# Block-local attention: every other step issued in reverse order on TensorE

## Chip, cores, metric

One core of a Trainium2 chip. The metric is the device time of one execution in microseconds (us). TensorE multiplies matrices (its weight load is a separate instruction), VectorE and ScalarE and GpSimd work on elements, and SyncE only issues the DMAs. In the rows PE is TensorE, PEld its weight loads, DVE is VectorE, ACT is ScalarE, POOL is GpSimd, SP is SyncE and SPq its queue of DMA issues. Each engine works through its own instructions strictly in the order of the program and waits for others by semaphores.

## What is computed

An attention layer is followed by two feed-forward layers; only the attention is touched. Shapes: 2 batches, 8 heads, 768 positions, 64 channels per head.

```python
k_sum = k.reshape(B, H, nb, block, D).max(axis=3)        # 24 blocks of 32
v_sum = v.reshape(B, H, nb, block, D).mean(axis=3)
scores_l = scale * q @ k^T, kept where |i - j| < 16, else -1e9
scores_s = scale * q @ k_sum^T + log(32)
a = softmax(concat(scores_l, scores_s))
x = a @ concat(v, v_sum)                                  # -> 1536 tokens x 512
x = moe(x)      # h = x @ w_in;  (h * cos h) @ w_out
return moe2(x)  # h = x @ w_in2; (h * softmax h), layer norm, @ w_out2
```

## The kernel before

Attention runs over 8 pairs of heads (pair n), and each pair over 3 groups of queries, so there are 24 groups G = 3n + g. A group is four tiles of 64 queries for both heads of its pair; a tile meets a window of 96 keys and the 24 block columns, 120 columns (KW) in all. The loop `for step in range(NGR + LA)` (29 steps) is a software pipeline written by hand: in one step each engine works on another stage of another group, and the order of the Python lines is the order on each engine.

In step t TensorE issues, in this order: the scores of group t+1 (`emit_s`, L507; 16 products of 64 rows by 64 columns, two at a time), the transposes of the weights of group t-4 (`emit_t`, L544; 4 of 128 by 128), when g = 2 the transposes of k and q of pair n+2 (L443, L479), from step 15 on three or four products of the first feed-forward layer (`fill`, L234), the products with v of group t-5 (`emit_av`, L562; 16 of 120 rows by 64 columns), and in steps 1, 2, 4, 7, 10, 13, 16, 19 the block sums of v of a pair (`sum_v`, L421; 24 of 96 rows by 64 columns).

VectorE in step t does the softmax sum of group t-2, when g = 0 the block maxima of k (L455), the masked maximum of group t (`emit_max`, L518), the last part of a weight conversion (`weights.finish`, L171), and when g = 1 copies of k and q (`pair_k`, `pair_q`, L375). GpSimd does `weights.split` (L187), the subtraction of the maximum (L522), the normalisation of group t-2 (L537), and the low half of a chunk of X (`split_x`, L204). ScalarE does the high half of a weight block (L186), the exponential of group t-1 (L527), the first part of a weight conversion (`weights.rebias`, L163 and L164), the copy of the transposed weights out of PSUM (`emit_at`, L552), the copy of the group's result to X (`emit_x`, L576), when g = 0 the key and query layouts of the next pair (`emit_kx`, `emit_qx`, L464 to L493), the high half of `split_x` (L203), and the scaling of the block sums (`scale_v`, L429). From group 20 (copy of weights) and 19 (copy to X) on, the two copies are VectorE's.

SyncE's queue gets in a step: the loads of weight blocks (`weights.bits`, L139, in the steps of `WSTEPS`, each one block ahead), when g = 1 the loads of k and q of pair n+3 and of v of pair n+2 (`load_v`, four DMAs, L389 and L393), and one step after `sum_v` the DMAs that put the block means beside v (`place_vsum`, L436). The weight block asked for in step 9 is the first one.

Four buffers hold v ("vt"), so `load_v(4)` in step 7 takes the buffer of pair 0 and `load_v(6)` in step 13 that of pair 2; its DMAs wait until the last product with v of that pair, groups 2 and 8. `emit_s` uses two PSUM banks in turn, `emit_t` one bank, `emit_av` one bank, which the copies give free. The block sums of pairs 6 and 7 use the PSUM space of the transposes of k and q. After step 28 TensorE goes on with the feed-forward layers; the products of the first of them need chunks of X that `split_x` makes in the steps of `XS`.

Of the kernel before, what the change touches and what calls it, by code (L numbers as in the profile page):

```python
# [7 lines left out]
F32 = mybir.dt.float32  # L8
# [12 lines left out]
QT = 64  # L21
# [13 lines left out]
def fused_kernel(  # L35
# [15 lines left out]
    P = 128  # L51
# [7 lines left out]
    KW = WIN + NS  # L59
    NG = 4  # L60
# [25 lines left out]
    def bank(i, name):  # L86
        return ps.tile([P, 512], F32, tag=f"m{i}", name=name)
# [4 lines left out]
    wide = w_in.dtype == mybir.dt.int64  # L92
    LOWEST = -3.0e38
    WSTEPS = (9, 10, 12, 13, 15, 17, 18, 19)
    XS = (7, 10, 13, 16)
    IDLE = (0, 0, 0)
    DVE_AT = 20
    DVE_X = 19
# [201 lines left out]
    def warm_up(n):  # L300

        if not n:
            return
        t = ps_h0.tile([P, 512], F32, tag="h", name="idle")
        for _ in range(n):
            nc.tensor.matmul(t, lhsT=idle[:, 0:P], rhs=idle, start=True, stop=True)
# [28 lines left out]
    def attention():  # L335
        st = ExitStack()
        with st:
            io = st.enter_context(tc.tile_pool(name="io", bufs=2))
            fix = st.enter_context(tc.tile_pool(name="fix", bufs=1))
            sm_p = st.enter_context(tc.tile_pool(name="sm", bufs=6))  # L340
# [24 lines left out]
            def load_k(n):  # L365
                k_t[n] = load_heads(k, n, "kt", 2)
# [11 lines left out]
            def pair_k(n):  # L378
                k_t[n] = side_by_side(k_t[n], "kg", False)

            def pair_q(n):
                q_t[n] = side_by_side(q_t[n], "qg", n < 2)
# [27 lines left out]
            def blocks_of(t):  # L410
                at = FIRST if t == 0 else FINAL if t == NT - 1 else MID + 2 * HALF - 2 * (t % HALF)
                return strip[0:WIN, at:at + D]

            def sum_v(n):

                o = (ps_h0 if n < 6 else ps_qk).tile(
                    [P, 512] if n < 6 else [P, 2, 2, S // 2], F32, tag="h" if n < 6 else "qk", name="vsum")
                o = (o if n < 6 else o[:, 0, 0])[:, 0:P]
                for t in range(HALF):
                    for c in range(2):  # L420
                        nc.tensor.matmul(  # L421
                            o[D * c:D * c + D], lhsT=blocks_of(HALF * c + t),
                            rhs=v_t[n][0:WIN, HALF * c + t].rearrange("p j d -> p (j d)"),
                            start=(t == 0), stop=(t == HALF - 1))
                vs_t[n] = o
# [21 lines left out]
            def emit_k(n):  # L447
                qk = ps_qk.tile([P, 2, 2, S // 2], F32, tag="qk", name="qk")
                transposed(k_t.pop(n), qk[:, 0, 0], qk[:, 0, 1])
                qk_t["k", n] = qk[:, 0]  # L450
                qk_t["q", n] = qk[:, 1, 0], qk[:, 1, 1]
# [45 lines left out]
            sm_t, at_t, ss_t, o_t, sum_t = {}, {}, {}, {}, {}  # L497

            def emit_s(G):
                n, g = divmod(G, GPP)  # L500
                qx, kx = kx_t[n]
                sps = bank(G % 2, "sps").rearrange("p (i s) -> p i s", i=NG)[:, :, 0:KW]
                for i in range(NG):
                    t = NG * g + i
                    for j in range(2):
                        h = slice(D * j, D * j + D)
                        nc.tensor.matmul(  # L507
                            sps[h, i, :], lhsT=qx[h, t * QT:(t + 1) * QT], rhs=kx[h, t, :],
                            start=True, stop=True)
                ss_t[G] = sps  # L510

            def emit_max(G):
                g = G % GPP
                sm = sm_t[G] = sms[G % NSM]
                sps = ss_t.pop(G)
                mx = sm_p.tile([P, NG], F32, tag="mx", name="mx")
                for i in range(NG):
                    nc.vector.tensor_tensor_reduce(  # L518
                        out=sm[:, i, 0:KW], in0=sps[:, i, :], in1=mask[:, g + i, :], scale=1.0, scalar=LOWEST,
                        op0=ALU.add, op1=ALU.max, accum_out=mx[:, i:i + 1])  # L520
                sm = sm[:, :, 0:KW]
                nc.gpsimd.tensor_tensor(  # L522
                    out=sm, in0=sm, in1=mx.unsqueeze(2).to_broadcast([P, NG, KW]), op=ALU.subtract)
# [21 lines left out]
                at_t[G] = aps  # L545

            def emit_at(G):
                at = sm_p.tile([KW, NG, P], F32, tag="at", name="at", bufs=2)
                if G >= DVE_AT:
                    nc.vector.tensor_copy(at, at_t[G])  # L550
                else:
                    nc.scalar.activation(out=at, in_=at_t[G], func=AF.Copy)  # L552
                at_t[G] = at

            def emit_av(G):
                n, g = divmod(G, GPP)
                b, hp = divmod(n, NP)
                at, vt = at_t.pop(G), v_t[n]
                ops = bank(3, "ops").rearrange("p (i s) -> p i s", i=NG)[:, :, 0:QT]
                for i in range(NG):  # L560
                    for j in range(2):
                        nc.tensor.matmul(  # L562
                            ops[64 * j:64 * j + 64, i, :], lhsT=vt[0:KW, NG * g + i, j, :],
                            rhs=at[:, i, 64 * j:64 * j + 64], start=True, stop=True)
                o_t[G] = ops

            def emit_x(G):
                n, g = divmod(G, GPP)
                b, hp = divmod(n, NP)
                ops = o_t.pop(G)  # L570
                c0 = b * S + g * NG * QT
                dst = X[:, hp, c0:c0 + NG * QT].rearrange("p (i s) -> p i s", i=NG)
                if G >= DVE_X:
                    nc.vector.tensor_copy(dst, ops)
                else:
                    nc.scalar.activation(out=dst, in_=ops, func=AF.Copy)  # L576

            NPAIR = B * NP
            NGR = NPAIR * GPP
# [25 lines left out]
            LX, LN, LT, LA = 1, 2, 4, 5  # L605
            VSUM_AT = {1: 0, 2: 1, **{3 * m - 2: m for m in range(2, NPAIR)}}
            for step in range(NGR + LA):
                n, g = divmod(step, GPP)
                summed = LN <= step < NGR + LN
                ahead = n + 1 if g == 0 and n + 1 < NPAIR else 0  # L610

                warm_up(IDLE[g] if step < min(FILL) else 0)
                if step + 1 < NGR:
                    emit_s(step + 1)
                if step == 0:
                    emit_max(0)
                    pair_k(1)
                    pair_q(1)
                    emit_k(1)
                    emit_q(1)  # L620
                if LT <= step < NGR + LT:
                    emit_t(step - LT)
                if g == 2 and n + 2 < NPAIR:
                    emit_k(n + 2)
                    emit_q(n + 2)
                fill(step)
                if step >= LA:
                    emit_av(step - LA)
                if step in VSUM_AT:
                    sum_v(VSUM_AT[step])  # L630

                weights.split()
                if LX <= step < NGR + LX:
                    emit_exp(step - LX)
                if summed:
                    emit_sum(step - LN)
                if ahead and step:
                    emit_ksum(ahead)
                weights.rebias()
                if 0 < step < NGR:  # L640
                    emit_max(step)
                if ahead and not step:
                    emit_ksum(ahead)
                drain(step - NGR)
                if LT <= step < NGR + LT:
                    emit_at(step - LT)
                weights.finish()
                if summed:
                    emit_norm(step - LN)
                if step >= LA:  # L650
                    emit_x(step - LA)
                if ahead:
                    emit_kx(ahead)
                    emit_qx(ahead)
                if step in WSTEPS:
                    weights.bits()
                for c in range(KC):
                    if step == XS[c]:
                        xs_of[0, c] = split_x(0, c, xs_a)
                if g == 1 and n + 2 < NPAIR:  # L660
                    pair_k(n + 2)
                    pair_q(n + 2)

                if g == 1 and n + 3 < NPAIR:
                    load_k(n + 3)
                    load_q(n + 3)
                if g == 1 and n + 2 < NPAIR:
                    load_v(n + 2)
                if step - 1 in VSUM_AT:
                    place_vsum(VSUM_AT[step - 1])  # L670
                if step in VSUM_AT:
                    scale_v(VSUM_AT[step])
# [303 lines left out]
```

## Time and profile before

| what | us |
|---|---|
| median of 3 runs (lowest to highest) | 494.49 (492.2 to 495.02) |
| the profiled execution | 492.56 |
| its span on the core | 490.8 |
| TensorE busy in the span | 477.8 (97%) |
| attention, up to the first product of `emit_y` (L276) | 103.0 |
| feed-forward layers behind it | 387.8 |

The busy time says how much of the span an engine had an instruction at work. From 103 us on TensorE has hardly a gap; all else that it lacks lies in the attention stage, where four engines and the DMA queues hand work to each other. So the stage has to be read by its waits, step by step: the timeline of each engine there, and the chain of waits that ended last.

### The profile page before, as it was taken

The numbers are of one execution on the slowest core, as the hardware profiler recorded it, in microseconds if no ns is written. First come the engines' busy times: TensorE is split into PE (matmuls) and PEld (weight loads), VectorE is DVE, ScalarE is ACT, GpSimd is POOL, SyncE is SP. The second block draws the span as 40 slices with busy tenths as digits, with TensorE's granted clock in tenths as the row PEclk, the third lists the DMA queues.
The fourth block names the chain that finished last, engine by engine and source line by source line (L and its number), as shares of the span: only waits on it lengthen the run. The fifth ranks groups of instructions, "written<-read, shape, count | busy, mean of one in ns | idle before, by whom it ended". The sixth has DMA issues, their size and how long they took to land.

```text
span 490.8 us, 7868 instructions
## 1 busy us (share of the span) xinstructions
PE 477.8 (97%) x2938; PEld 392.4 (80%) x2938; DVE 299.8 (61%) x667; ACT 314.1 (64%) x540; POOL 149.8 (31%) x144
## 2 busy tenths in 40 slices
PE   8899799999999999999999999999999999999997
PEld 4787687778888888888888888888888888888886
DVE  3895876773455456556564664556477776776661
ACT  3578889646685766556656653788624867777621
POOL 0586998622422222222222220245500011110000
PEclk9999999999999999999999999999999999999999
DMA  8888872201223322332233221220001333224201
GB/s 248 204 220 252 235 191 58 106 2 43 87 85 97 118 85 87 92 124 85 85 98 116 87 85 39 90 87 1 0 1 43 87 87 86 66 64 65 70 37 44
DMA packets 59046, 46.17 MB, mean 94 GB/s; under 512 B 40448, under 2 KB 51328, under 8 KB 59008
## 3 DMA queue, kind: packets, MB, share of 16 engines
q1 hardware_dynamic: 59008, 45.67, 32.4%
q8 instruction: 23, 0.38, 0.3%
q14 instruction: 15, 0.12, 0.1%
HBM read 36.61 MB, written 3.15 MB: 81 GB/s over the span
## 4 chain that ended last, share of the span: by engine, by line
PE 87%; ACT 3%; POOL 3%; DVE 3%; DMA 2%; issue 1%; SPq 0%; ACTq 0%; POOLq 0%
PE y L276 27%; PE h L234 26%; PE o L851 13%; PE h L737 13%; PE sps L507 2%; PE ops L562 1%; PE aps L544 1%; POOL sm L522 1%; PE vsum L421 1%; DMA qt<-in_q_dram 1%; DMA raw<-in_moe_w_in_dram 1%; POOL sm L537 1%; POOL w L187 1%; ACT kx L464 1%; PE qk L443 1%
## 5 line engine op out<-in xcount | busy, mean ns | idle before, releaser
L234 PE MATMUL h<-xs,w 128*128 128x512 f32 x576 | 141.2, 391 | 0.0
L276 PE MATMUL y<-gs,w 128*128 128x512 f32 x576 | 138.2, 389 | 0.0
L276 PEld LDWEIGHTS y<-gs,w 128*128 128x128 f32 x576 | 108.0, 188 | 22.5
L234 PEld LDWEIGHTS h<-xs,w 128*128 128x128 f32 x576 | 107.1, 188 | 21.6
L187 POOL TENSOR_TENSOR w<-s,w 128x512 fp32r<-128x512 f32 x48 | 62.5, 1302 | 157.8 <-ACT w L186 134.8
L243 ACT ACTIVATE r<-h 128x512 int32<-128x512 f32 x48 | 28.6, 596 | 85.9 <-PE h L234 85.9
L248 DVE SCALAR_TENSOR_TENSOR r<-r,h 128x512 f32<-128x512 int32 x48 | 32.9, 685 | 67.2 <-ACT r L243 67.1
L171 DVE SCALAR_TENSOR_TENSOR s<-raw 128x512 int32<-128x512 int32 x48 | 36.7, 764 | 52.3 <-ACT raw L164 44.1
L851 PE MATMUL o<-w,ls 128*128 128x512 f32 (+1 forms) x312 | 67.8, 373 | 0.0
L737 PE MATMUL h<-w,xs 128*128 128x512 f32 x288 | 67.6, 390 | 0.0
L851 PEld LDWEIGHTS o<-w,ls 128*128 128x128 f32 x312 | 55.3, 188 | 10.7 <-DVE ls L827 0.4
L737 PEld LDWEIGHTS h<-w,xs 128*128 128x128 f32 x288 | 53.9, 188 | 11.1
L204 POOL TENSOR_TENSOR xs<-X,xs 128x512 fp32r<-128x512 f32 x22 | 30.6, 1398 | 37.6 <-ACT xs L203 37.6
L772 POOL TENSOR_TENSOR st<-st,mhalf 128x1 f32<-128x1 f32 x12 | 6.6, 550 | 110.1 <-DVE st L771 100.0
L253 ACT ACTIVATE r<-r,half_pi 128x512 f32<-128x512 f32 x48 | 34.5, 718 | 1.6 <-DVE r L248 1.6
L264 DVE TENSOR_TENSOR gs<-h,gs 128x512 fp32r<-128x512 f32 x48 | 32.6, 679 | 4.2 <-ACT gs L263 4.0
L258 DVE TENSOR_TENSOR h<-h,r 128x512 f32<-128x512 f32 x48 | 32.9, 685 | 0.4 <-ACT r L253 0.4
L163 ACT ACTIVATE raw<-raw 128x512 f32<-128x512 f32 x48 | 31.8, 662 | 0.6 <-DMA raw<-in_moe_w_in_dram 0.6
L164 ACT ACTIVATE raw<-raw 128x512 int32<-128x512 uint32 x48 | 31.8, 663 | 0.0
L522 POOL TENSOR_TENSOR sm<-sm,mx 128x480 f32<-128x480 f32 x24 | 25.6, 1065 | 19.4 <-DVE mx L518 19.4
L186 ACT ACTIVATE w<-s 128x512 fp32r<-128x512 f32 x48 | 30.1, 626 | 1.8 <-DVE s L171 1.5
L754 ACT ACTIVATE e<-h,st 128x1024 f32<-128x1024 f32 (+1 forms) x13 | 13.6, 1049 | 26.3 <-DVE st L750 22.9
(79 smaller groups left out, 560.9 us busy)
## 6 DMA issues: line engine op xcount, KB each, us to landing
raw<-in_moe_w_in_dram SPq DMA_DIRECT2D x24, 512.0 KB, 3.9
raw<-in_moe_w_out_dram SPq DMA_DIRECT2D x24, 512.0 KB, 3.3
vt<-in_v_dram SPq DMA_DIRECT2D x16, 240.0 KB, 4.9
kt<-in_k_dram SPq DMA_DIRECT2D x8, 384.0 KB, 3.7
qt<-in_q_dram SPq DMA_DIRECT2D x8, 384.0 KB, 4.0
out_dram<-osb SPq DMA_DIRECT2D x11, 256.0 KB, 2.0
vt<-vm SPq DMA_DIRECT2D x16, 72.0 KB
vt<-in_v_dram SPq DMA_DIRECT2D x16, 48.0 KB, 5.6
```

What stands on the lines that cost most here:

```text
L163: nc.scalar.activation(out=hw, in_=hw, func=AF.Prelu, scale=REBIAS, alpha=NEGATIVE)
L164: nc.scalar.activation(out=lw, in_=lw.bitcast(U32), func=AF.Copy, scale=TOP3)
L171: nc.vector.scalar_tensor_tensor(out=self.f32[i], in0=t[:, :, 1], scalar=3, in1=t[:, :, 0], op0=ALU.logical_shift_left, op1=ALU.bitwise_or)
L187: nc.gpsimd.tensor_tensor(out=w[:, 1, :], in0=f, in1=as32(w[:, 0, :]), op=ALU.subtract)
L234: nc.tensor.matmul(h, lhsT=w[:, a, f * P:(f + 1) * P], rhs=xs_of[tb, c][:, b_, :], start=(m == 0), stop=(m == 3 * KC - 1))
L248: nc.vector.scalar_tensor_tensor(out=r, in0=r.bitcast(I32), scalar=TWO_PI, in1=h_of[step], op0=ALU.mult, op1=ALU.subtract)
L253: nc.scalar.activation(out=r, in_=r, func=AF.Sin, scale=-1.0, bias=half_pi)
L258: nc.vector.tensor_tensor(out=h, in0=h, in1=r, op=ALU.mult)
L264: nc.vector.tensor_tensor(out=gs[:, 1, :], in0=r, in1=as32(gs[:, 0, :]), op=ALU.subtract)
L276: nc.tensor.matmul(y[e], lhsT=w[:, a, e * P:(e + 1) * P], rhs=gs[:, b_, :], start=(f == 0 and i == 0), stop=(f == GF - 1 and i == 2))
L737: nc.tensor.matmul(banks[n], lhsT=xs_of[NTB + t // TPB, c][:, a, t0:t0 + P], rhs=weights.done[w2i[c][n]][:, b_, :], start=(m == 0), stop=( ...
L851: nc.tensor.matmul(o, lhsT=ls_of[t][f // 4][:, a, s0:s0 + P], rhs=w[:, b_, cols], start=(f == 0 and i == 0), stop=(f == NF2 - 1 and i == 2))
```

## The change

Even steps keep their order on TensorE, odd steps run it backwards, and the products with v of two groups are issued together in the even step. Even step t: scores of t+1, transposes of t-4, (k and q), fill, products with v of t-6 and of t-5, block sums. Odd step t: block sums, transposes of t-4, (k and q), fill, scores of t+1. The results of two groups share one PSUM bank, and both are copied to X in the odd step that follows (`emit_x`). The transposed weights get a third buffer. Two chunks of X are split one step later (`XS`).

```diff
-    XS = (7, 10, 13, 16)
+    XS = (7, 11, 13, 17)
...
-                at = sm_p.tile([KW, NG, P], F32, tag="at", name="at", bufs=2)
+                at = sm_p.tile([KW, NG, P], F32, tag="at", name="at", bufs=3)
...
-                ops = bank(3, "ops").rearrange("p (i s) -> p i s", i=NG)[:, :, 0:QT]
+                if G % 2 == 0:
+                    o_t["bank"] = bank(3, "ops").rearrange("p (a i s) -> p a i s", a=2, i=NG)
+                ops = o_t["bank"][:, G % 2]
...
-                if step + 1 < NGR:
+                odd = step % 2
+                if step + 1 < NGR and not odd:
                     emit_s(step + 1)
+                if odd and step in VSUM_AT:
+                    sum_v(VSUM_AT[step])
...
                 fill(step)
-                if step >= LA:
+                if odd and step + 1 < NGR:
+                    emit_s(step + 1)
+                if not odd and step > LA:
+                    emit_av(step - LA - 1)
                     emit_av(step - LA)
-                if step in VSUM_AT:
+                if not odd and step in VSUM_AT:
                     sum_v(VSUM_AT[step])
...
-                if step >= LA:
-                    emit_x(step - LA)
+                if step > LA and (odd or step == NGR + LA - 1):
+                    end = step - LA + 1 - odd
+                    emit_x(end - 2)
+                    emit_x(end - 1)
```

## Rows read from the trace of the kernel before

**Rows 1.** Busy time by stretch: us, each engine (instructions), PEclk, DMA share, GB/s

```profile
110.00:135.00 25.00, 25.00 (x112) 20.68 (x112) 10.71 (x16) 17.07 (x32) 8.32 (x7) 1.00 0.20 64
```

**Rows 2.** Chain of waits, in order of time: start us, us, what

```profile
39.82 3.90 DMA raw<-in_moe_w_in_dram
...
86.19 1.04 PE sps L507 x16
...
102.96 5.67 PE y L276 x24
```

**Rows 3.** Timeline of TensorE, steps 3 to 8: start us, us, instruction, [idle before]

```profile
21.43 1.86 PE L507 MATMUL sps<-kx,qx 64*64 64x120 f32 x32
...
28.74 1.04 PE L507 MATMUL sps<-kx,qx 64*64 64x120 f32 x16
29.71 0.65 PE L544 MATMUL aps<-ident,sm 128*120 128x128 f32 x4
30.29 0.69 PE L562 MATMUL ops<-at,vt 120*64 120x64 f32 x16
30.90 1.04 PE L507 MATMUL sps<-kx,qx 64*64 64x120 f32 x16
...
32.97 1.48 PE L421 MATMUL vsum<-vt,strip 96*64 96x128 f32 x24
...
37.24 0.69 PE L562 MATMUL ops<-at,vt 120*64 120x64 f32 x16
```

**Rows 4.** Timeline of SyncE's issues, 28 to 40 us

```profile
28.26 1.73 SPq L393 DMA_DIRECT2D vt<-in_v_dram  x1
...
33.18 0.34 SPq L389 DMA_DIRECT2D vt<-in_v_dram  x1
...
38.10 1.67 SPq L436 DMA_DIRECT2D vt<-vm  x2
39.82 1.50 SPq L139 DMA_DIRECT2D raw<-in_moe_w_in_dram  x3
```

**Rows 5.** View of the tile vt: from issue of its DMAs to landing

```profile
DMA to landing us min/median/max: 3.4/5.5/6.8
```

**Rows 6.** DMA issues of the page: KB each, median us from issue to landing

```profile
raw<-in_moe_w_in_dram SPq DMA_DIRECT2D x24, 512.0 KB, 3.9
...
qt<-in_q_dram SPq DMA_DIRECT2D x8, 384.0 KB, 4.0
```

**Rows 7.** Timeline of SyncE's issues, 66 to 69 us

```profile
66.61 0.32 SPq L389 DMA_DIRECT2D vt<-in_v_dram  x1
...
68.73 0.40 SPq L139 DMA_DIRECT2D raw<-in_moe_w_out_dram  x1
```

**Rows 8.** Timeline of ScalarE, 43 to 78 us

```profile
43.74 0.67 ACT L163 ACTIVATE raw<-raw 128x512 f32<-128x512 f32 x1 [0.56 <-DMA raw<-in_moe_w_in_dram]
...
63.58 0.38 ACT L576 ACTIVATE X<-ops 128x256 f32<-128x256 f32 x1 [0.47 <-PE ops L562]
...
72.14 0.38 ACT L576 ACTIVATE X<-ops 128x256 f32<-128x256 f32 x1 [1.45 <-PE ops L562]
...
76.74 0.82 ACT L493 ACTIVATE qx<-qk 128x768 f32<-128x768 f32 x1
```

**Rows 9.** Timeline of GpSimd at 46 us

```profile
46.31 1.46 POOL L204 TENSOR_TENSOR xs<-X,xs 128x512 fp32r<-128x512 f32 x1 [3.23 <-ACT xs L203]
```

**Rows 10.** Timeline of VectorE, the maximum of group 20

```profile
81.64 0.28 DVE L518 CUSTOM_DVE_ANT_0 sm<-sps,mask 128x120 f32<-128x120 f32 x1
```

**Rows 11.** Timeline of VectorE, steps 24 to 27

```profile
93.64 0.42 DVE L574 COPY X<-ops 128x256 f32<-128x256 f32 x1 [0.86 <-PE ops L562]
...
101.11 0.68 DVE L550 COPY at<-aps 120x512 f32<-120x512 f32 x1
```

**Rows 12.** Timeline of VectorE, two copies of q

```profile
46.06 0.55 DVE L375 COPY qg<-qt 128x768 f32<-128x768 f32 x1
...
57.30 1.63 DVE L375 COPY qg<-qt 128x768 f32<-128x768 f32 x1
```

## The prediction

> **What bounds the kernel now.** I read the busy time by stretch first: from 110 us on TensorE is busy for the whole of a stretch [rows 1], and the attention stage ends where the first product of the feed-forward layer starts, at 102.96 [rows 2]. The change touches only what lies before, so its gain or loss is the shift of that point. Then the chain of waits of that stage: it does not stay on one engine. Up to 38 us it runs on TensorE, there it goes through SyncE's queue to the load of the first weight block [rows 2], then over ScalarE, GpSimd and VectorE, and it comes back to TensorE at 86.19 with the scores of group 23 [rows 2]. So time taken out of TensorE counts in full at the start and at the end of the stage, and in the middle only where TensorE is what the others wait for.
>
> **The price of a change of product.** Two groups of scores side by side are busy for 1.86 us, one for 1.04 [rows 3]: the second costs 0.82. Alone, scores occupy TensorE from 28.74 to 29.71, 0.97. The difference, 0.15 us, is what one change of kind costs. Products with v take 0.61 (30.29 to 30.90) and I take the same 0.15 for a second group of them, so 0.46. Before, two steps have six changes (scores, transposes, v, twice); after, four. I count 10 new pairs of scores (groups 2 and 3 wait for a layout in any case, 4 and 5 stand side by side already) and 12 pairs of products with v: 22 times 0.15 is 3.3 us of TensorE's work. It is the most that the change can give, if every bit lies on the path.
>
> **The first stretch, to step 8: nothing is left.** Four of the pairs lie here (-0.6). But in step 7 the block sums of pair 3 now come first. Before, they start at 32.97 without waiting, two blocks of products after the step's start at 30.90 [rows 3]. The last DMA of that v is issued at 28.26 [rows 4] and takes at least 3.4 us [rows 5], so it lands at 31.66 at the earliest; TensorE comes to it at some 30.9 and waits 0.8 or more (32.97 bounds it: 2.1). That takes back the 0.6. I take +0.1 for TensorE here.
>
> **SyncE's queue: the one moved wait.** `load_v(4)` of step 7 needs the buffer of pair 0, and the last reader of it, group 2's products with v, goes from step 7 to step 8. Before, the load starts at 33.18, right when they end [rows 4]. After, they stand in front of those of group 3, which start at 37.24 [rows 3]; without group 2's own 0.61 in step 7, and with half a block of them to run, and the +0.1, they end at 37.2 to 37.9. I take 37.9: the load comes 4.7 us later. Behind it on the queue are `place_vsum(3)`, which nobody needs soon, and then the first weight block, which ScalarE does need. Before, the queue went from 33.18 to 39.82 in 6.6 us: 4.9 for the four DMAs of v, then 1.7 [rows 4]. The four are that slow because the queue was still full: the load of q just ahead takes 4.0 us to land [rows 6]. With the queue empty, the same four took 66.61 to 68.73, 2.1 us [rows 7]. The loads of k and q ahead are issued before 33.18 and so land by 37.2, and at 37.9 the queue is empty: 37.9 + 2.1 + 1.7 = 41.7 for the weight block against 39.82, **+1.9** (bounds: +1.4 if they end at 37.4; +4.7 if the queue takes 6.6 again). ScalarE stood ready 0.56 before the block landed at 43.72 [rows 8], so all of the delay is its idle time, and the other engines hang on it from here: GpSimd already stands 3.23 us before, waiting for ScalarE [rows 9]. Two effects hide in this shadow at no cost: the block sums of pair 5, now first in step 13, wait for a v that comes later too, where TensorE anyway waits for ScalarE; if that cover were thin, +0.7. `load_v(6)` moves likewise from step 13 to 14; the weight blocks behind it are each a block ahead, and its v is wanted only at the end of step 16: nothing.
>
> **XS.** The second chunk's split moves from step 10 to 11. On GpSimd it took 1.46 us in that idle time [rows 9]; in step 11 it stands in front of a weight block's low half and the next maximum. Between 0 and 1.46; I take half, **+0.7**. The fourth chunk (16 to 17) delays fill in step 18 on TensorE, which is idle shortly after: nothing.
>
> **ScalarE's waits for products with v.** Before, its copy to X waits for products of the same step: 0.47 at 63.58 and 1.45 at 72.14, where TensorE has k, q and fill in front [rows 8]. After, the copies come one step behind the products and wait for nothing: **-1.9**, in steps where ScalarE has nothing else free. Waits like these before 43 us don't count, as ScalarE then waits for the weight block.
>
> **Step 19.** Block sums of pair 7 now come first and need the space that `emit_qx(7)` frees at 77.56 (76.74 + 0.82) [rows 8]. TensorE comes to them some 2.2 us sooner than before, the time of one step's scores, transposes and products with v (28.74 to 30.90) [rows 3], stands as long, then needs 1.5 for the sums, 0.6 and 1.0 for transposes and scores: group 20's scores end at 80.6. They are wanted at 81.64 [rows 10]: hidden, by 1.0 us. If not, up to +1.5.
>
> **The end of the stage.** From 86.19 four pairs of products with v save 0.6. But VectorE's chain of the activation bounds these steps too, down to the last copy of weights at 101.11; its copy of group 19, which waited 0.86 for TensorE at 93.64 [rows 11], leaves step 24, and those of 20 and 21 leave steps 25 and 26. Between 0 and -1.5; I take **-0.7**.
>
> **Sum.** +0.1 + 1.9 + 0.7 - 1.9 - 0.7 = +0.1 us on the profiled execution's own 492.56 (span 490.8, 1.8 around it). That execution lies 1.9 under the median of the runs, 494.49, and I set the forecast beside the median: **494.5 us**, with its own range from 492.5 to 496.5 from the terms' bounds.
>
> **Rivals.**
>
> A. *All of TensorE's saving arrives* (-3.0 of the 3.3): the late weight block is made up in steps 10 to 18 by ScalarE and TensorE together. For it: TensorE is without a gap in long parts of the stage. Against: the chain leaves it between 39 and 86 us. 491.5.
>
> B. *The weight block comes 4.7 late, not 1.9*: slower. The place is SyncE's queue in step 8, the price the 4.9 us for four DMAs [rows 4] instead of 2.1 [rows 7], so +2.8; it decides as soon as these issues take over 4 us. Against it stands the empty queue, for it that only the last of the eight loads of v went that quickly. 497.3.
>
> C. *VectorE's copies of q lose their place to GpSimd.* In step 10 one takes 0.55, started just ahead of GpSimd's work; in step 13, with GpSimd at work, 1.63 [rows 12]. The change shifts both engines against each other; if the two quick ones of steps 10 and 16 become slow, two times 1.08 lies on VectorE's queue ahead of weight conversion: +2.2, 496.7. The Trainium skill has this as a rule (Advanced Engine Details and Errata, VectorE Performance Modes: VectorE's second port is GpSimd's too, and copies that use it and GpSimd's instructions block each other); the trace agrees by 0.55 and 1.63.
>
> D. *The change doesn't do what it says.* The second scores of a pair wait for the maximum two groups back, the second transposes for the copy of the first, with only products with v or a fill between: if such waits part the pairs, the saving of the last stretch falls away and some is lost. 495.7.
>
> **How the numbers follow.** Forecast 0.48, A 0.13, B 0.16, C 0.12, D 0.11. About 0.5%, 2.5 us, is what a measurement of this kernel can tell from no change. Faster (under 492.0): most of A and a little of the forecast's edge, 0.13. Slower (over 497.0): most of B and under half of C, 0.18. Same: 0.69. The range holds the forecast's, C and D and half of A and B: 491.4 to 497.6.
>
> **What would show it.** Right: scores in pairs of 1.86 us and products with v in pairs near 1.15; `load_v(4)` at about 37.9 and the first weight load at about 41.7; ScalarE's wait for it near 2.4 instead of 0.56; no wait of its copies to X for TensorE; TensorE standing some 2 us ahead of the last block sums; the first product of `emit_y` within 1.5 us of 102.96. Wrong: the weight block's load before 40.5 or after 43; scores in step 20 later than 81.6; over 1 us of waits of transposes for copies in steps 23 to 28, which I have priced at nothing. Anything that differs behind 103 us would be outside this reasoning.

## The result, and the profile after

| what | before | after |
|---|---|---|
| median of 7 runs (lowest to highest), us | 495.02 (491.98 to 495.62) | 497.26 (496.10 to 501.12) |
| ratio to before, 95% interval | | 1.0077 (1.0055 to 1.0100) |
| the profiled execution, us | 492.56 | 496.10 |
| its span, us | 490.8 | 494.3 |
| first weight conversion on ScalarE (L163) starts at | 43.74 | 47.41 |
| first product of `emit_y` in the chain of waits at | 102.96 | 106.46 |
| feed-forward layers behind it (span less the line above) | 387.8 | 387.8 |

The change makes the kernel slower, by more than 0.5%. (The medians of the seven runs are 2.2 us apart, their means, 497.94 and 494.25, 3.7; the ratio rests on all the runs.) Medians here and below are of all runs of a kernel; ratios leave out one run of e9_late_weights, 798.03 us at a granted clock of 0.56.

In the two profiled executions all of it lies where the prediction looked for it: the span grew by 3.5 us, the first product of `emit_y` comes 3.5 us later, and what follows takes as long as before. Inside the attention stage there is one more dividing line, the first weight conversion. Up to there the changed kernel is 47.41 - 43.74 = 3.67 us later; 0.36 of that lies ahead of step 3's scores (21.79 against 21.43). From there to the first product of `emit_y` it gives back 0.17 (106.46 - 47.41 = 59.05 against 102.96 - 43.74 = 59.22).

The chain of waits of the changed kernel (start us, us, what) where it leaves TensorE, and its end:

```profile
38.33 1.08 PE ops L564 x32
39.41 0.60 PE aps L544 x4
40.03 0.60 ACT at L552
41.19 0.77 SPq L436
...
42.84 4.55 DMA raw<-in_moe_w_in_dram
...
104.42 0.75 DVE X L576 x2
105.31 1.15 PE ops L564 x32
106.46 5.69 PE y L276 x24
```

The same load of the first weight block stands in it as in [rows 2], at 42.84 instead of 39.82 and for 4.55 us instead of 3.90. New is the last link: a copy of X on VectorE releases the last pair of products with v. (The view puts a copy of weights ahead of SyncE's `place_vsum`; what the queue stood for is seen in its own timeline.)

SyncE's issues of the changed kernel from 32 to 43 us (start us, us, instruction):

```profile
32.66 0.53 SPq L357 DMA_DIRECT2D qt<-in_q_dram  x1
38.99 0.34 SPq L389 DMA_DIRECT2D vt<-in_v_dram  x1
...
40.47 0.56 SPq L393 DMA_DIRECT2D vt<-in_v_dram  x1
41.12 1.67 SPq L436 DMA_DIRECT2D vt<-vm  x2
42.84 2.43 SPq L139 DMA_DIRECT2D raw<-in_moe_w_in_dram  x3
```

From 33.19 to 38.99 the queue issues nothing: `load_v(4)` stands in front and waits for the buffer. Before, it started at 33.18 [rows 4]. Then the four DMAs take 38.99 to 41.12, 2.13 us, `place_vsum(3)` 1.72, and the weight block goes out at 42.84.

TensorE's timeline of the changed kernel (start us, us, instruction, xcount, [idle before <-releaser]):

```profile
30.21 1.15 PE L564 MATMUL ops<-at,vt 120*64 120x64 f32 x32
32.44 1.62 PE L421 MATMUL vsum<-vt,strip 96*64 96x128 f32 x24 [1.08 <-DMA vt<-in_v_dram]
...
34.58 1.86 PE L507 MATMUL sps<-kx,qx 64*64 64x120 f32 x32
...
38.26 1.15 PE L564 MATMUL ops<-at,vt 120*64 120x64 f32 x32
...
49.22 1.08 PE L544 MATMUL aps<-ident,sm 128*120 128x128 f32 x4 [4.01 <-ACT at L552]
...
67.92 1.04 PE L507 MATMUL sps<-kx,qx 64*64 64x120 f32 x16 [0.55 <-DVE mx L518]
...
80.95 1.60 PE L421 MATMUL vsum<-vt,strip 96*64 96x128 f32 x24 [0.43 <-ACT qx L493]
...
105.31 1.15 PE L564 MATMUL ops<-at,vt 120*64 120x64 f32 x32 [0.76 <-DVE X L576]
106.39 3.94 PE L276 MATMUL y<-gs,w 128*128 128x512 f32 x16
```

The change does what it says: pairs of products with v of 1.15 us, pairs of scores of 1.86. One pair of scores is parted: those of groups 16 and 17, where the second waits 0.55 us at 67.92 for VectorE's maximum. The products of groups 2 and 3 at 38.26 are those that `load_v(4)` waits for. Ahead of them, in step 7, TensorE stands 1.08 us for the v of pair 3. And it stands 4.01 us at 49.22 with the others, because ScalarE is late.

ScalarE's waits, by what it waited for: us in total, times, longest. First the changed kernel, 47.4 to 80.8 us, then the kernel before in the same steps, 43.7 to 77.5 us:

```profile
ACT raw L163 <- DMA raw<-in_moe_w_in_dram: 3.6, 1, 3.6
ACT w L186 <- DVE s L171: 1.4, 1, 1.4
ACT sm L527 <- POOL sm L522: 1.2, 2, 1.0
ACT at L552 <- PE aps L544: 1.1, 1, 1.1
ACT vm L429 <- PE vsum L421: 0.4, 1, 0.4
```

```profile
ACT X L576 <- PE ops L562: 2.8, 3, 1.5
ACT sm L527 <- POOL sm L522: 0.7, 3, 0.3
ACT w L186 <- DVE s L171: 0.6, 2, 0.3
ACT raw L163 <- DMA raw<-in_moe_w_in_dram: 0.6, 1, 0.6
```

The first line of each list that is about `raw` is the wait ahead of the stretch. Without it ScalarE waited 4.1 us before and 4.1 us after. The 2.8 us for products with v are gone as predicted, and other waits of the same sum stand in their place.

### The profile page after: what moved, and what is told of

Read it like the earlier page. It is cut to its first block, busy times and chain, and to the rows that moved or that the text cites. A ratio compares the mean times of both kernels' runs of the same rounds, so it can differ in the third digit from the quotient of the medians.

```text
span 494.3 us, 7867 instructions
## 1 busy us (share of the span) xinstructions
PE 476.1 (96%) x2938; PEld 393.0 (80%) x2938; DVE 300.1 (61%) x667; ACT 314.1 (64%) x540; POOL 149.0 (30%) x144
## 3 DMA queue, kind: packets, MB, share of 16 engines
HBM read 36.61 MB, written 3.15 MB: 80 GB/s over the span
## 4 chain that ended last, share of the span: by engine, by line
PE 85%; ACT 5%; DVE 4%; DMA 3%; SPq 1%; issue 1%; POOL 1%; POOLq 0%; ACTq 0%
PE y L276 26%; PE h L234 25%; PE o L861 13%; PE h L747 13%; PE sps L507 2%; PE aps L544 1%; DMA qt<-in_q_dram 1%; DMA raw<-in_moe_w_in_dram 1%; PE ops L564 1%; DMA vt<-in_v_dram 1%; ACT sm L527 1%; ACT kx L464 1%; DVE sm L518 1%; POOL sm L522 1%; ACT at L552 1%
## 5 line engine op out<-in xcount | busy, mean ns | idle before, releaser
L276 PE MATMUL y<-gs,w 128*128 128x512 f32 x576 | 138.2, 389 | 0.0
L276 PEld LDWEIGHTS y<-gs,w 128*128 128x128 f32 x576 | 108.0, 188 | 22.5
L204 POOL TENSOR_TENSOR xs<-X,xs 128x512 fp32r<-128x512 f32 x22 | 29.6, 1354 | 36.2 <-ACT xs L203 36.2
L163 ACT ACTIVATE raw<-raw 128x512 f32<-128x512 f32 x48 | 31.8, 663 | 3.6 <-DMA raw<-in_moe_w_in_dram 3.6
L764 ACT ACTIVATE e<-h,st 128x1024 f32<-128x1024 f32 (+1 forms) x13 | 13.6, 1049 | 26.6 <-DVE st L760 23.2
```

Source lines behind the costliest of these rows:

```text
L163: nc.scalar.activation(out=hw, in_=hw, func=AF.Prelu, scale=REBIAS, alpha=NEGATIVE)
L276: nc.tensor.matmul(y[e], lhsT=w[:, a, e * P:(e + 1) * P], rhs=gs[:, b_, :], start=(f == 0 and i == 0), stop=(f == GF - 1 and i == 2))
```

## The experiments

Two theories for the 3.67 us, which don't exclude each other. **The queue:** group 2's products with v, moved from step 7 to step 8, hold pair 0's buffer, SyncE's queue stands, and the weight block behind that load is late. **TensorE's first stretch:** the block sums of pair 3, now first in step 7, wait for their v and delay everything behind them, the queue included. For the second half of the stage: why it gave back 0.2 and not the 1.9 + 0.7 that the prediction had, less XS.

One remark on reading single profiles: the scores of step 3 start anywhere between 20.1 and 23.2 us in the fourteen profiles, and a profiled execution can be among the slowest of its kernel. So I compare stretches, and medians of 8 to 12 runs each with 31 runs of the kernel before on the same chip (median 493.96 in the first group of runs, 494.64 in the second, 494.04 in the third).

### A fifth buffer for v (e1_five_v), and the same in the kernel before (b1_five_v)

```diff
-                t = io.tile([P, NT, 2, D], F32, tag="vt", name="vt", bufs=4)
+                t = io.tile([P, NT, 2, D], F32, tag="vt", name="vt", bufs=5)
```

> The changed kernel with five buffers for v instead of four, so that the load of pair 4's v in step 7 and of pair 6's in step 13 wait for no product. Theory 1 (the moved wait on SyncE's queue makes the loss, by the late first weight block): the load starts at about 33.2 instead of 38.99, the first weight block's load at 38 to 40.5 instead of 42.84, ScalarE waits under 1 us for it instead of 3.56, TensorE stays at 2.4 GHz, and the stage ends at 102 to 103 instead of 106.4: 3 to 4 us less than the changed kernel, level with the kernel before or up to 1 us under it. Theory 2 (the reversed order itself makes the loss: block sums that wait for v and for the key layout, copies to X that hold the bank): the queue is early, but the stage still ends after 105.

> The kernel before with five buffers for v. There the loads of v wait 0.2 and 2.7 us for products, the longer one late in the stage where no engine needs the data soon. Theory 1 expects no gain: the stage ends within 0.3 us of 102.96, so that the gain of five buffers in the changed kernel is the moved wait alone. Rival (five buffers are worth something by themselves): 0.5 us or more earlier.

Measured: e1_five_v 493.73, ratio 0.9989 (0.9955 to 1.0024); b1_five_v 493.12, ratio 0.9981 (0.9953 to 1.0009). SyncE's issues and ScalarE's first conversion in e1_five_v, from their timelines:

```profile
33.04 0.46 SPq L389 DMA_DIRECT2D vt<-in_v_dram  x1
...
39.34 1.49 SPq L139 DMA_DIRECT2D raw<-in_moe_w_in_dram  x3
```

```profile
44.59 0.70 ACT L163 ACTIVATE raw<-raw 128x512 f32<-128x512 f32 x1
```

With the buffer the queue doesn't stand: `load_v(4)` is issued at 33.04, the weight block at 39.34 (6.3 us from one to the other, near the 6.6 of [rows 4]: 3.8 for the four DMAs, 0.8 in which the placing waits for ScalarE, 1.7 for the placing), and ScalarE converts without waiting for it. No loss is left that the runs can tell; the stage of this execution ends at 103.50, with step 3 starting 1.4 us later than in the kernel before. In the old order the fifth buffer makes no difference that can be measured, so it isn't a gain of its own that hides a loss: the buffer is worth something only because the change needs it. (The profiled execution of b1_five_v, the slowest of its ten runs, ends the stage at 106.54 and not within 0.3 us of 102.96 as expected.) But neither is there a gain left of TensorE's 3.3 us.

### The weight block ahead of v (e2_weights_first), and the same in the kernel before (b2_weights_first)

```diff
+                if step == 7:
+                    weights.load(0)
+                    weights.load(1)
                 if g == 1 and n + 3 < NPAIR:
```

> The changed kernel with the loads of the first two weight blocks issued in step 7, ahead of the loads of k, q and v of that step; the load of pair 4's v waits as in the changed kernel. Theory 1 (late weight block): ScalarE waits for no weight block in step 10, the stage ends at 102 to 103.5. Rival 1b (it is the late v, not the late weight block): v of pairs 4 and 5 comes later still, block sums of pair 5 stand for it in step 13, and the stage ends after 105.

> The kernel before with the first two weight blocks' loads ahead of the loads of step 7. In the kernel before ScalarE waits 0.56 us for the block; Theory 1 expects no more than that, 0 to 0.6 us, to be gained, and 59.2 us from the first conversion to the end of the stage. If the kernel before too has more to gain by an early block: over 0.3% faster.

Measured: e2_weights_first 492.81, ratio 0.9978 (0.9947 to 1.0009); b2_weights_first 493.42, ratio 0.9987 (0.9961 to 1.0013). Here pair 0's buffer comes still later than in the changed kernel (the load of v goes out at 41.65, 20.4 us after the start of step 3's scores, against 17.2), but the weight block doesn't stand behind it. SyncE, TensorE and ScalarE in e2_weights_first:

```profile
33.22 1.03 SPq L139 DMA_DIRECT2D raw<-in_moe_w_in_dram  x2
```

```profile
33.49 1.62 PE L421 MATMUL vsum<-vt,strip 96*64 96x128 f32 x24 [2.25 <-DMA vt<-in_v_dram]
...
35.95 3.15 PE L507 MATMUL sps<-kx,qx 64*64 64x120 f32 x32
```

```profile
46.37 0.69 ACT L163 ACTIVATE raw<-raw 128x512 f32<-128x512 f32 x1
```

The loss is gone in the runs, which agrees with the queue: it is what stands behind the load that costs, more than the late v. The profile shows the second theory's wait beside it, and misses what was expected of it. In this execution, the second slowest of ten (494.98), the block sums wait 2.25 us for v, the pair of scores after that takes 3.15 us instead of 1.86, and the conversion starts at 46.37 although nothing waits for weights: that is 25.1 us after step 3's scores, against 25.6 in the changed kernel and 22.3 before. The delay is in the steps themselves now, and the stage ends at 105.31. So a long wait for v in step 7 costs about as much without the queue; how often it is that long, the runs don't say.

### Only a late weight block, in the old order (e9_late_weights), beside the changed kernel again (a2_changed)

```diff
+                if step == 9:
+                    late = fix.tile([P, 1], F32, name="late")
+                    nc.sync.dma_start(out=late, in_=kx_t[4][0][:, 0:1])
                 if step in WSTEPS:
```

A small DMA that waits for the query layout of pair 4 stands ahead of the first weight block on SyncE's queue; everything else is the kernel before.

> The kernel before, in its own order, with one small DMA (4 bytes from each partition of the query layout of pair 4 to an unused tile) ahead of the first weight block's load on SyncE's queue; it waits until ScalarE has written that layout in step 9, so the weight load is late by about 3.4 us and nothing else is changed. Theory 1 (the late weight block alone makes the loss): load at 43 instead of 39.8, conversion at about 47, from there 59.2 us as before, so the stage ends 3 to 3.6 us later and the kernel is 0.5 to 0.8% slower, as the changed one. Rival (later slack takes the delay up in this order): less than half of it arrives at the end of the stage.

> The changed kernel once more, on the chip and in the rounds of the three others. Theory 1: slower than the kernel before by 0.4 to 0.9%, ScalarE's first weight conversion waits 2.5 us or more for its load, and from there to the end of the stage 58.9 to 59.1 us.

Measured: e9_late_weights 497.79, ratio 1.0057 (1.0036 to 1.0078); a2_changed 497.35, ratio 1.0056 (1.0027 to 1.0085). SyncE, ScalarE and TensorE in e9_late_weights:

```profile
43.87 0.55 SPq L657 DMA_DIRECT2D late<-qx  x1
44.47 1.54 SPq L139 DMA_DIRECT2D raw<-in_moe_w_in_dram  x3
```

```profile
48.45 0.65 ACT L163 ACTIVATE raw<-raw 128x512 f32<-128x512 f32 x1 [4.11 <-DMA raw<-in_moe_w_in_dram]
```

```profile
108.64 3.69 PE L276 MATMUL y<-gs,w 128*128 128x512 f32 x15
```

A late weight block alone makes a loss of the changed kernel's size, with no reversed step at all. It is not the same dose: here the block is issued 22.9 us after the start of step 3's scores (21.59), against 18.4 before and 21.1 in the changed kernel. From the conversion to the first product of `emit_y` it takes 60.19 us, not the 59.2 expected (before: 59.15, counted to the same row), so in this execution nothing of the delay is made up. In the runs 0.57% arrives, 2.8 us, less than the 4.5 by which this profile's block is late; how late it is in the other runs isn't known. So e9_late_weights shows that such a delay comes through, not that the two kernels agree to a tenth.

The changed kernel in a2_changed, profiled in its slowest of twelve runs (499.50):

```profile
33.65 2.67 PE L421 MATMUL vsum<-vt,strip 96*64 96x128 f32 x24 [2.64 <-DMA vt<-in_v_dram]
...
37.30 3.47 PE L507 MATMUL sps<-kx,qx 64*64 64x120 f32 x32
```

```profile
47.23 1.81 SPq L139 DMA_DIRECT2D raw<-in_moe_w_in_dram  x3
```

Here the two theories act together. The sums wait 2.64 us where they waited 1.08 in the first profile, TensorE then works at a granted clock of 0.50 (35 to 40 us), `load_v(4)` goes out 21.9 us after step 3's scores instead of 17.2, and the weight block behind it 25.8 instead of 21.1. The wait of the sums, and the slower products behind it, set how late the queue is. The two executions of the changed kernel are 3.4 us apart; from step 3's scores to the first product of `emit_y` it is 3.7 (88.34 against 84.60), so their difference lies here.

### Block sums in even steps, behind the products with v (e7_sums_even)

```diff
-            VSUM_AT = {1: 0, 2: 1, **{3 * m - 2: m for m in range(2, NPAIR)}}
+            VSUM_AT = {1: 0, 2: 1, 4: 2, 8: 3, 10: 4, 14: 5, 16: 6, 19: 7}
```

> The changed kernel with the block sums of pairs 3 and 5 one step later, at the end of the even steps 8 and 14, instead of first in the odd steps 7 and 13 (four buffers for v, as in the changed kernel). Theory 1b (part of the late weight block comes from the block sums of pair 3 that wait 1.1 us and more for v in step 7): no such wait, products with v of group 2 end at about 37 instead of 38.8, the four loads of v start at about 37.3 and the weight block's at 41.2 instead of 42.84; ScalarE starts the conversion at 45.5 to 46.3 instead of 47.41 and the stage ends 1.1 to 1.9 earlier than in the changed kernel. Rival (the wait is hidden behind the queue): the load starts after 38.5 and the end stays within 0.5.

Measured: 494.42, ratio 0.9995 (0.9968 to 1.0023). With the sums of pair 3 moved from the front of step 7 to the end of step 8, `load_v(4)` starts 15.0 us after step 3's scores instead of 17.2, and the weight block goes out at 39.68, 17.8 us after them instead of 21.1. Of these 3.2 us, 2.2 are the earlier load; the rest is that `place_vsum(3)`, 1.7 us, now follows the weight block, less 0.6 because the four issues take longer. So the sums and their wait for v are a large part of what kept group 2's products back: 2.2 of the 5.4 us by which the load was later than before (17.2 against 33.18 - 21.43 = 11.75). But the edit has a price of its own, and from the conversion to the first product of `emit_y` this kernel takes 60.35 instead of 58.98 (each counted to TensorE's first row of L276). ScalarE's timeline:

```profile
64.26 0.28 ACT L429 ACTIVATE vm<-vsum 128x128 f32<-128x128 f32 x1 [3.58 <-PE vsum L421]
```

The block sums of pair 5, moved from the front of step 13 to the end of step 14, make ScalarE wait 3.58 us.

### Cover for TensorE's idle time (e4_busy)

With TensorE idle for 4.01 us, its granted clock falls. Busy time by stretch in the changed kernel: stretch, length, busy us of PE, PEld, DVE, ACT, POOL (instructions), granted clock, DMA share, GB/s:

```profile
50.00:51.00 1.00, 1.00 (x7) 1.00 (x6) 0.96 (x4) 1.00 (x3) 0.94 (x1) 0.50 1.10 358
```

A granted clock of 0.50 is the lower of its two levels, 1.2 GHz. To see what it costs, idle products are put into the gap:

```diff
+                warm_up(16 if step == 10 else 0)
                 if not odd and step in VSUM_AT:
```

> The changed kernel with 16 idle products (128 by 512, results unused) on TensorE in step 10, ahead of the block sums of pair 4, where TensorE otherwise stands for 4.0 us while ScalarE waits for the weight block. If the clock's fall to 1.2 GHz between 49.4 and 52.6 us is part of the loss: the granted clock stays at 1.0 in that stretch, transposes of k and q in step 11 take 0.85 each instead of 1.49 and 1.44, and the stage ends 0.7 to 1.3 us earlier. If the slow transposes are hidden behind ScalarE and VectorE: clock up, end within 0.3 of 106.4.

Measured: 496.63, ratio 1.0048 (1.0016 to 1.0080). The same stretch in e4_busy, and TensorE's first product of `emit_y`:

```profile
50.00:51.00 1.00, 1.00 (x11) 1.00 (x10) 0.97 (x4) 1.00 (x3) 0.98 (x1) 1.00 1.04 341
```

```profile
106.24 3.93 PE L276 MATMUL y<-gs,w 128*128 128x512 f32 x16
```

The clock is back at 1.00 and the stage isn't shorter: 106.24 - 47.31 = 58.93 us from the conversion on, against 106.39 - 47.41 = 58.98. In this place the lower clock lies beside the work of the engines that are late anyway. In step 7 it doesn't: there it delays `load_v(4)`, as a2_changed showed.

### All copies of X on ScalarE (e5_x_scalar), and the same with a fifth buffer in the kernel before (b4_all)

```diff
-    DVE_X = 19
+    DVE_X = 99
```

> The changed kernel with all copies to X on ScalarE (before and in the changed kernel those of groups 19 to 23 are VectorE's). If the 0.76 us that the last products with v wait for VectorE's copies of groups 20 and 21 is a loss of its own: no such wait, the stage ends 0.5 to 1.0 earlier. Rival (VectorE's chain of the activation sets that end anyway): within 0.3.

> The kernel before with five buffers for v and all copies to X on ScalarE, against which the reversed order with the same two edits is to be held. In the kernel before one copy (group 19) waits 0.86 us on VectorE for products with v; on ScalarE the copies of groups 19 to 23 leave VectorE's chain of the activation: 0.3 to 1.2 us earlier than 102.96. If ScalarE becomes late instead: within 0.3 or later.

Measured: e5_x_scalar 494.95, ratio 1.0021 (0.9990 to 1.0052); b4_all 494.18, ratio 1.0006 (0.9980 to 1.0032). TensorE at the end of the stage in e5_x_scalar, and in b4_all:

```profile
106.89 1.15 PE L564 MATMUL ops<-at,vt 120*64 120x64 f32 x32
107.97 1.43 PE L276 MATMUL y<-gs,w 128*128 128x512 f32 x5
```

```profile
100.27 0.62 PE L544 MATMUL aps<-ident,sm 128*120 128x128 f32 x4 [1.29 <-DVE at L550]
```

The last pair of products with v no longer waits for its bank. From the last query layout on ScalarE (`emit_qx(7)`) to the first product of `emit_y` it takes 25.45 us instead of 26.31 in the changed kernel and 26.15 in the kernel before: with this the 0.7 that the prediction had for the end of the stage is there. In the old order the same edit works the other way, 26.70 us against 26.15; there transposes wait 1.29 us for VectorE. The runs of e5_x_scalar lie between the changed kernel and the kernel before, and the interval takes in no change; that the edit is worth 0.9 us rests on the profiles. It takes work off VectorE besides, so the 0.9 isn't the bank's wait alone.

### Three edits, and four (e8_all, e10_best)

e8_all is the changed kernel with the fifth buffer, e7_sums_even's order and `DVE_X = 99`. e10_best takes the weights first as well, and moves pair 5's sums to step 13 again, since they made ScalarE wait:

```diff
+            VSUM_AT = {1: 0, 2: 1, 4: 2, 8: 3, 10: 4, 13: 5, 16: 6, 19: 7}
```

> The changed kernel with five buffers for v, the block sums of pairs 3 and 5 at the end of steps 8 and 14, and all copies to X on ScalarE: the three suspected losses taken away together. If they are the losses and they add up: from the start of ScalarE's first weight conversion to the end of the stage 58.1 us (59.2 in the kernel before), that start at or before 43.7, the end of the stage at 101 to 102.2, 1 to 2 us less than the kernel before. If a saved wait is taken by the next engine again: within 0.5 us of the kernel before.

> The changed kernel with five buffers for v, the first two weight blocks' loads ahead of the loads of step 7, the block sums of pair 3 at the end of step 8, and all copies to X on ScalarE. If the losses are the late weight block, TensorE's wait for v in step 7 and the bank held by VectorE's copies: no wait of ScalarE for the weight block, 57.9 to 58.2 us from the first conversion to the end of the stage, 0.4 to 0.8% faster than the kernel before. If the queue's order only moves the wait to the loads of v behind it: block sums of pairs 4 or 5 wait over 1 us, and within 0.3% of the kernel before.

Measured: e8_all 492.97, ratio 0.9962 (0.9945 to 0.9978); e10_best 491.12 (488.99 to 492.65), ratio 0.9934 (0.9907 to 0.9961), below both kernels. ScalarE in e8_all, then SyncE, ScalarE and TensorE in e10_best:

```profile
47.93 0.65 ACT L163 ACTIVATE raw<-raw 128x512 f32<-128x512 f32 x1 [3.44 <-DMA raw<-in_moe_w_in_dram]
```

```profile
31.91 1.02 SPq L139 DMA_DIRECT2D raw<-in_moe_w_in_dram  x2
```

```profile
41.50 0.70 ACT L163 ACTIVATE raw<-raw 128x512 f32<-128x512 f32 x1
```

```profile
42.70 1.60 PE L421 MATMUL vsum<-vt,strip 96*64 96x128 f32 x24 [1.52 <-DMA vt<-in_v_dram]
...
52.09 2.43 PE L421 MATMUL vsum<-vt,strip 96*64 96x128 f32 x24 [2.44 <-DMA vt<-in_v_dram]
...
100.68 3.69 PE L276 MATMUL y<-gs,w 128*128 128x512 f32 x15
```

In e8_all the runs are faster, but the profile, the slowest of its ten (495.57), isn't what was expected: the weight block is issued 18.4 us after step 3's scores, as in the kernel before, and ScalarE still waits 3.44 us for it, because it takes 6.3 us to come; why is open. From there on the 57.94 us are as expected (58.1).

In e10_best the conversion starts at 41.50 without a wait. From there to the first product of `emit_y` it takes 59.18 us and not the 57.9 to 58.2 expected. What remains of the queue's trouble has moved to v itself: the block sums of pairs 4 and 5 now wait 1.52 and 2.44 us for it. So the reversed order can end 0.66% below the kernel before, once the queue, the sums and the last copies are arranged for it. In the old order the fifth buffer, the weights first, and the fifth buffer with the copies on ScalarE gave no difference that can be measured. The last of these, b4_all (1.0006), is e8_all (0.9962) without the change and without its order of the sums. All four edits together weren't run in the old order, so how much of the 0.66% belongs to the reversal, and how much to which edit, stays open.

## Why the prediction was wrong, by its own steps

The forecast was 494.5 us and no change that can be measured; the kernel got slower by 0.77% (0.55 to 1.00). The sum was +0.1; the profiled execution shows +3.5. Three terms are short of it: the queue by 1.7 us, ScalarE's waits with XS by 0.9, the end of the stage by 0.9.

**The queue: the right mechanism, mis-sized.** The prediction had +1.9 for the late weight block plus +0.1 for TensorE's first stretch; the conversion came 3.67 later, and e1_five_v, e9_late_weights and the runs of e2_weights_first show the mechanism. Its working was right where it had rows: the four issues after the standstill 2.13 us for 2.1 [rows 7], the placing 1.72 for 1.7. It was short in two places. The load started at 38.99 and not at 37.9: this execution is 0.36 later from step 3 on, the wait of the block sums was 1.08 and not the 0.8 that I called its least, and transposes in step 5 stand 0.28 for their copy, 0.9 of the 1.1 in all. I took the bottom of that wait's bounds (0.8 to 2.1) and gave its spread no price on the queue; other profiles of the reversed order with these sums in step 7 have 0.89 to 2.65. Other executions have the conversion later still: from step 3's scores to the conversion it took 25.6 us here, 26.7 in e4_busy and 29.5 in a2_changed (22.3 before). And the block took 4.57 us from issue to ScalarE's start where I had carried over the 3.9 of [rows 6]: the v of pair 4 went out directly ahead of it, when before it had a longer lead. That this is why it landed later is argued, not shown; the landings in the other kernels (3.75 in a2_changed to 6.33 in e8_all, from issue to conversion) don't sort by it. 1.9 + 1.1 + 0.65 makes the 3.67 but for rounding.

**ScalarE's waits for products with v, -1.9: the step that failed.** The waits of `emit_x` went as forecast, 2.8 us of them, and nothing was won: from the first conversion to `emit_qx(7)` the stage took 32.67 us instead of 33.00 (80.08 and 76.74 [rows 8] less the two conversions), -0.3 where I had -1.9 and +0.7 for XS, -1.2 together. (The 2.8 have a third wait, 0.86 at 60.52, that I hadn't listed.) ScalarE's queue is a list in which the next entry waits too: for GpSimd's subtraction, VectorE's last part of a conversion, the transposes. I gave the removed wait its full length without asking what stood behind it. XS was not tested by itself: the 0.3 is the two terms together.

**The end of the stage, -0.7: taken by a wait that I hadn't listed.** It came out at +0.2 (26.31 us from `emit_qx(7)` on, against 26.15). Two groups share one PSUM bank now, and the next pair of products can begin only when VectorE has copied both halves. At 105.31 that is 0.76 us of waiting. I had listed the copies of 20 and 21 as leaving steps 25 and 26, and not asked who waits for them where they arrive. Without that wait, in e5_x_scalar, it is 25.45 us, a gain of the size that I had, though there VectorE has less to do besides.

**What held.** The price of a pair of scores and of products with v; that step 19 costs nothing, though TensorE stood 0.43 us ahead of the sums of pair 7 (at 80.95) and not some 2; everything behind the attention stage. `load_v(6)` cost nothing either, and it is the longer standstill: the queue waited for it from 56.94 to 64.69, 7.7 us, and no conversion behind it waited for a weight block, since these are a block ahead. The first weight load was to come between 40.5 and 43 and came at 42.84, near the end, and ScalarE's wait of 3.56 instead of 2.4 says the same. Group 20's scores start at 83.06, after the 81.6 that I had named as a sign of being wrong, but the whole stage is later by then and VectorE takes them up at 84.98 only.

**The rivals.** B gave 497.3, and the result is 497.26, but B didn't happen: it was to decide when the four issues take over 4 us, and they took 2.13. The number agrees by other terms. C didn't happen either; VectorE's copies of q in steps 10 and 16 stayed at 0.55 us. Nor D in the last stretch, though one pair was parted before it, by 0.55 us at 67.92 and by the wait that D names. A's time, 491.5, was reached only with four further edits (e10_best, 491.12). What I should have priced as a rival is the sum I made with the two gains left out: +0.1 + 1.9 + 0.7 is +2.7, 497.2, slower. Both of them rested on a removed wait not being replaced, and I gave them the weight of a measured row.

## What to carry to other kernels

Where a reader is moved to a later step, look up who refills its buffer, and then what stands behind that refill on the same queue: the loss here came from a weight block that has nothing to do with the change. A wait that is taken out of an engine's list is worth its length only up to the next wait in that list; write down the next one before you count the gain. And where two results share a bank, the wait for the bank is that for the later of its two copies.

## What the runs showed of the hardware

The same four loads of v (`load_v(4)`) took 2.0 to 2.1 us to issue after the queue had stood for 5.7 us and more, in five profiles of the reversed order, and 3.8 to 5.8 right behind the loads of k and q (33.04 to 36.83 in e1_five_v, 32.64 to 38.40 in b4_all). A standstill alone doesn't settle it: the first profile of the changed kernel has `load_v(6)` go out from 64.69 to 68.50, 3.8 us, after 7.7 us in which the queue stood.

```profile
64.69 0.34 SPq L389 DMA_DIRECT2D vt<-in_v_dram  x1
...
65.69 2.20 SPq L389 DMA_DIRECT2D vt<-in_v_dram  x1
```

So an empty queue, which the prediction gave as the reason, is at least not the whole of it. An earlier load doesn't bring the entry behind it forward by as much as it moves itself: counted from step 3's scores, e1_five_v issues `load_v(4)` 7.0 us sooner than the changed kernel and the weight block 4.6 us sooner.

TensorE's granted clock fell to the 1.2 GHz level after 4.0 us without work, and in e2_weights_first after a wait of 2.25 us too, where the next pair of scores took 3.15 us instead of 1.86 (granted clock 0.50 from 36 to 38 us). What this costs depends on who waits for TensorE: in e4_busy, where idle products kept the level up in step 10, the stage was no shorter; in step 7 of a2_changed the slower products held `load_v(4)` back.
